# Half-masked score columns left out, with swapped token halves for the second batch entry

## The chip, the cores and the metric

The kernel runs on one core of a Trainium2 chip. A core has five engines that work side by side: TensorE (PE in the profile; matrix products, with the weight loads listed as PEld), VectorE (DVE), ScalarE (ACT), GpSimd (POOL) and SyncE (SP). TensorE writes into PSUM, of which this kernel uses eight banks of 128 x 512 float32 values; the others work on PSUM and on the on-chip SBUF. Sixteen DMA engines move data between the chip's main memory and SBUF; a load is issued by one of the engines, and in this kernel nearly all loads are issued by GpSimd[...].

The metric is device time in microseconds (us) for one launch; lower is better.

## The reference

Two layers follow each other. The first is a retention (linear attention with decay) over 4 batch entries, 8 heads, 768 tokens and 64 values per head. The second is a feed-forward block with a sigmoid gate on the 3072 token rows.

```python
# q, k, v: (4, 8, 768, 64)
gamma = 1.0 - 2.0 ** (-5.0 - np.arange(H))          # one decay per head
for t in range(S):
    state = gamma[None, :, None, None] * state + np.einsum('bhd,bhe->bhde', k[:, :, t], v[:, :, t])
    y[:, :, t] = scale * np.einsum('bhd,bhde->bhe', q[:, :, t], state)
...
x = y.transpose(0, 2, 1, 3).reshape(B * S, H * D)   # (3072, 512)
gate = 1.0 / (1.0 + np.exp(-(x @ w_gate)))          # w_gate, w_val: (512, 1536)
out = (gate * (x @ w_val)) @ w_out                  # w_out: (1536, 512)
```

The kernel doesn't step token by token. It cuts the 768 tokens into 6 chunks of 128 (C). Inside a chunk it forms the scores of each key token against each query token, multiplies them with a table that holds the decay and is zero where the key is later than the query (the causal mask), and multiplies the result with v ("intra"). What comes from earlier chunks goes through a 64 x 64 state per head ("inter").

## The kernel before

A "pair" is one chunk t of two batch entries: pair i stands for chunk i // 2 and entries 2 (i % 2) and 2 (i % 2) + 1, so there are 12 pairs. Pairs 0 and 1 have code of their own at the start; pairs 2 to 11 go through the code below. j is the entry within the pair, p one of four couples of heads, e the head within the couple. D = 64, H = 8, NP = 4, NT = 6. `half(x)` is partitions 0 to 63 or 64 to 127.

Loads, issued by GpSimd. Rows of 64 values are the unit that a load moves in these patterns. For the second entry the two heads of each couple change places, hence three loads for k and three for q.

```python
    def load_v(i):
        t, h = divmod(i, 2)
        vs[i] = ld.tile([C, 2 * H, D], BF16, tag="vs", name="vs", bufs=6)
        nc.gpsimd.dma_start(out=vs[i], in_=v[2 * h:2 * h + 2, :, t * C:(t + 1) * C, :].rearrange("b h s d -> s (b h) d"))

    def load_swapped(tiles, x, i, tag, bufs):
        t, h = divmod(i, 2)
        tiles[i] = ld.tile([C, 2 * H, D], BF16, tag=tag, name=tag, bufs=bufs)
        src = x[2 * h:2 * h + 2, :, t * C:(t + 1) * C, :].rearrange("b h s d -> b s h d")
        nc.gpsimd.dma_start(out=tiles[i][:, 0:H], in_=src[0])
        dst = tiles[i][:, H:2 * H].rearrange("s (p e) d -> s e p d", e=2)
        pairs = src[1].rearrange("s (p e) d -> s e p d", e=2)
        for e in range(2):
            nc.gpsimd.dma_start(out=dst[:, e], in_=pairs[:, 1 - e])

    def load_kq(i):
        load_swapped(kn, k, i, "kn", 6)
        load_swapped(qn, q, i, "qn", 4)
```

Tables. `maskk` is the causal mask times the decay of the key's token; `tabsk` holds the decay per key token, chunk and head.

```python
    def later_constants():
        nc.vector.tensor_scalar(tok, begin, ahead[:, 0:1], None, op0=ALU.add)
        tab_power(tok, 0, NT)
        shape = [128, NT, 2, NP]
        nc.vector.tensor_tensor(tabz, lgz.unsqueeze(1).to_broadcast(shape),
                                begin.unsqueeze(2).unsqueeze(3).to_broadcast(shape), op=ALU.mult)
# ... (later_exps: tabs and tabz go through Exp on ScalarE)
    def last_constants():
        nc.vector.tensor_scalar(causal, ahead, 0.0, None, op0=ALU.is_le)

    def later_tables():
        src = tabs[:, :, 0:NT].rearrange("s (p e) t -> s e t p", e=2)
        dst = tabsk.rearrange("s t j (p e) -> s j e t p", e=2)
        for j in range(2):
            for e in range(2):
                nc.gpsimd.tensor_copy(dst[:, j, e], src[:, e ^ j])
        for e in range(2):
            nc.gpsimd.tensor_tensor(maskk[:, e], causal.unsqueeze(1).to_broadcast([128, NP, C]),
                                    tabsk[:, 0, e, 0::2].unsqueeze(2).to_broadcast([128, NP, C]), op=ALU.mult)
```

The steps of a pair. For a product the first operand after the output is the stationary one (the weights), the second streams: its columns are what TensorE spends time on. A stationary operand of 64 partitions by 64 columns takes one quarter of the array, so four such products can run beside each other. The transposed k and q (`kqT`) come from DMA transposes (`xbar`), except for pair 2, where TensorE transposes.

```python
    def xbar(i):
        kqT[i] = at.tile([128, 2, 2, NP, C], BF16, tag="kqX", name="kqX", bufs=4)
        for which, x in enumerate((kn[i], qn[i])):
            nc.sync.dma_start_transpose(out=kqT[i][:, which].rearrange("d j p s -> d (j p) s"),
                                        in_=x.rearrange("s h d -> s (h d)"))

    def scale_k(i):
        ks[i] = ld.tile([C, 2 * H, D], BF16, tag="ks", name="ks", bufs=3)
        nc.gpsimd.tensor_tensor(ks[i], kn[i], tabsk[:, i // 2].rearrange("s j h -> s (j h)").unsqueeze(2)
                                .to_broadcast([C, 2 * H, D]), op=ALU.mult)
# ...
    def quarter_scores(i, j):

        t = kqT[i]
        sc[i, j] = (bank([128, NP, C]), bank([128, NP, C]))
        for p in range(NP):
            for g in range(2):
                for e in range(2):
                    nc.tensor.matmul(sc[i, j][e][half(g), p, :], t[half(e), 0, j, p, half(g)], t[half(e), 1, j, p, :],
                                     start=True, stop=True)

    def mask(i, j, e):
        st = stB if e else stA
        st[i, j] = at.tile([128, NP, C], BF16, tag=f"st{e}", name=f"st{e}", bufs=4)
        nc.vector.tensor_tensor(st[i, j], sc[i, j][e], maskk[:, e ^ j], op=ALU.mult)
# ...
    def intra(i, j):
        for p in range(NP):
            for e in range(2):
                st = (stA, stB)[e ^ j][i, j]
                nc.tensor.matmul(y[i, j][half(e), p, :], vs[i][:, j * H + 2 * p + e, :], st[:, p, :],
                                 start=False, stop=True, skip_group_check=True)
# ...
    def state(i):
        zz[i] = bank([128, 2, NP, D])
        for j in range(2):
            for p in range(NP):
                for e in range(2):
                    nc.tensor.matmul(zz[i][half(e), j, p, :], ks[i][:, j * H + 2 * p + e, :],
                                     vs[i][:, j * H + 2 * p + (e ^ j), :],
                                     start=(j == 0 and p == 0), stop=True, skip_group_check=True)
# ...
    def block(old, new, st=None):

        if old is not None:
            new_y(old)
            inter(old)
        for j in range(2):
            if new is not None:
                quarter_scores(new, j)
        for j in range(2):
            if old is not None:
                intra(old, j)
        if st is not None:
            state(st)
        for j in range(2):
            if old is not None:
                y_out(old, j)
        for j in range(2):
            if new is not None:
                mask(new, j, 0)
                mask(new, j, 1)
        if st is not None:
            state_sum(st)
```

Order of the program where pairs 2 to 6 come in. Every engine works through its own instructions in this order. `hold` is a one-column copy on GpSimd that keeps later loads from being issued before a pair's transposes are done. `plan` says after which group of the feed-forward products a step is put.

```python
    first_state(0)
    first_state(1)
    load_out(0)
    load_out(1)
    load_kq(2)
    load_out(2)
    load_out(3)
    load_v(2)
# ...
    def load_next(i):
        load_kq(i)
        load_v(i)

    held = const.tile([128, 1], BF16, name="held")

    def hold(i, which=1):
        nc.gpsimd.tensor_copy(held, kqT[i][:, which, 1, NP - 1, C - 1:C])

    load_next(3)
    scale_k(2)
    new_kqT(2)
    down(0, 0, 0, 6)
    transpose(2, 0)
    down(0, 1, 0, 6)
    transpose(2, 1)
    down(0, 2, 0, 6)
    for b in range(3):
        down(0, b, 6, 9)
    for j in range(2):
        quarter_scores(2, j)
        mask(2, j, 0)
        mask(2, j, 1)
    xbar(3)
    for b in range(3):
        down(0, b, 9, 12)
    scale_k(3)
    hold(3, 0)
    load_next(4)
    load_next(5)
    down(0, 3, 0, 6)
    new_y(2)
    inter(2)
    for j in range(2):
        intra(2, j)
    for j in range(2):
        y_out(2, j)
    state(2)
    state_sum(2)
    down(0, 3, 6, 12, True)
    casts(2)
# ...
    plan = {
        1: [(2, block, None, 3), (4, block, 3, None, 3), (4, xbar, 4), (4, scale_k, 4), (4, scale_k, 5), (4, hold, 4),
            (4, load_next, 6), (5, casts, 3), (7, xbar, 5), (11, block, None, 4, 4), (12, casts, 4), (12, xbar, 6), (12, scale_k, 6),
            (12, hold, 6), (12, load_next, 7), (14, block, 4, 5, 5), (16, casts, 5), (18, block, 5, 6, 6), (19, casts, 6)],
        2: [(0, xbar, 7), (0, scale_k, 7), (0, hold, 7), (0, load_next, 8), (8, block, 6, 7, 7), (10, casts, 7), (10, xbar, 8),
# ... (two blocks for each of chunks 2 to 4, with the loads of the pairs after them)
```

In the start-up, the states of pairs 0 and 1 (`first_state`) are formed by 64 products of 64 x 64 by 64 columns (line 396) and copied out of PSUM by four 128 x 256 copies (line 401). The first weight loads (line 79) bring 128 x 2 rows of 256 values each, the later ones 128 x 4.

The feed-forward products (`up` and `down`, line 411) run between these steps, and their results pass through ScalarE (sigmoid, line 437) and VectorE (gate times value, line 438).

Of the kernel before, what the change touches and what calls it, by code (L numbers as in the profile page):

```python
# [8 lines left out]
F32 = mybir.dt.float32  # L9
BF16 = mybir.dt.bfloat16  # L10
AX = mybir.ActivationFunctionType
ALU = mybir.AluOpType
# [3 lines left out]
def kernel(  # L16
# [9 lines left out]
):  # L26


    nc = tc.nc
    B, H, S, D = q.shape  # L30
    N_TOK, D_MODEL = out.shape
# [19 lines left out]

    def load_v(i):
        t, h = divmod(i, 2)
        vs[i] = ld.tile([C, 2 * H, D], BF16, tag="vs", name="vs", bufs=6)
        nc.gpsimd.dma_start(out=vs[i], in_=v[2 * h:2 * h + 2, :, t * C:(t + 1) * C, :].rearrange("b h s d -> s (b h) d"))  # L57

    def load_swapped(tiles, x, i, tag, bufs):
        t, h = divmod(i, 2)  # L60
        tiles[i] = ld.tile([C, 2 * H, D], BF16, tag=tag, name=tag, bufs=bufs)
        src = x[2 * h:2 * h + 2, :, t * C:(t + 1) * C, :].rearrange("b h s d -> b s h d")
        nc.gpsimd.dma_start(out=tiles[i][:, 0:H], in_=src[0])  # L63
        dst = tiles[i][:, H:2 * H].rearrange("s (p e) d -> s e p d", e=2)
        pairs = src[1].rearrange("s (p e) d -> s e p d", e=2)
        for e in range(2):
            nc.gpsimd.dma_start(out=dst[:, e], in_=pairs[:, 1 - e])  # L67

    def load_kq(i):
        load_swapped(kn, k, i, "kn", 6)  # L70
        load_swapped(qn, q, i, "qn", 4)

    wg = wpool.tile([128, KT, D_FF], BF16, name="wg")
    wv = wpool.tile([128, KT, D_FF], BF16, name="wv")
# [10 lines left out]
    def load_out(s):  # L85
        nc.gpsimd.dma_start(out=wo[:, s * 3:(s + 1) * 3, :],
                            in_=moe_w_out.rearrange("(n p) d -> p n d", p=128)[:, s * 3:(s + 1) * 3, :])
# [15 lines left out]
    nc.scalar.preload_act_table(AX.Exp)  # L103
    ahead = const.tile([128, C], F32, name="ahead")
    after = const.tile([128, 3, D], F32, name="after")
    tok = const.tile([128, NT], F32, name="tok")
    begin = const.tile([128, NT], F32, name="begin")
    col = const.tile([128, C], F32, name="col")
    nc.gpsimd.iota(ahead, pattern=[[-1, C]], base=0, channel_multiplier=1, allow_small_or_imprecise_dtypes=True)
# [20 lines left out]
    lgz = const.tile([128, 2, NP], F32, name="lgz")  # L130
    lsc = const.tile([128, 1], F32, name="lsc")
    ident = const.tile([128, 128], BF16, name="ident")
    causal = const.tile([128, 128], F32, name="causal")
    decay = const.tile([128, 2, 2, 2, 3 * D], F32, name="decay")
    maskk = const.tile([128, 2, NP, C], F32, name="maskk")
    tabs = const.tile([128, H, NT + 2], F32, name="tabs")
    tabsk = const.tile([128, NT, 2, H], F32, name="tabsk")
    taby = const.tile([128, NP, C], F32, name="taby")
    tabz = const.tile([128, NT, 2, NP], F32, name="tabz")
# [19 lines left out]
    def tab_power(x, lo, n):  # L159
        nc.vector.tensor_tensor(tabs_of[:, :, :, lo:lo + n], x.unsqueeze(1).unsqueeze(1).to_broadcast([128, NP, 2, n]),  # L160
                                nlg.rearrange("s e p -> s p e").unsqueeze(3).to_broadcast([128, NP, 2, n]), op=ALU.mult)
# [17 lines left out]
    nc.scalar.copy(kb[:, 4:8], kf[:, 4:8])  # L179

    def later_constants():
        nc.vector.tensor_scalar(tok, begin, ahead[:, 0:1], None, op0=ALU.add)
        tab_power(tok, 0, NT)
        shape = [128, NT, 2, NP]
        nc.vector.tensor_tensor(tabz, lgz.unsqueeze(1).to_broadcast(shape),
                                begin.unsqueeze(2).unsqueeze(3).to_broadcast(shape), op=ALU.mult)

    def later_exps():
        nc.scalar.activation(tabs, tabs, AX.Exp)
        nc.scalar.activation(tabz[:, 1:], tabz[:, 1:], AX.Exp)  # L190

    def last_constants():
        nc.vector.tensor_scalar(causal, ahead, 0.0, None, op0=ALU.is_le)

    def later_tables():
        src = tabs[:, :, 0:NT].rearrange("s (p e) t -> s e t p", e=2)
        dst = tabsk.rearrange("s t j (p e) -> s j e t p", e=2)
        for j in range(2):
            for e in range(2):
                nc.gpsimd.tensor_copy(dst[:, j, e], src[:, e ^ j])  # L200
        for e in range(2):
            nc.gpsimd.tensor_tensor(maskk[:, e], causal.unsqueeze(1).to_broadcast([128, NP, C]),
                                    tabsk[:, 0, e, 0::2].unsqueeze(2).to_broadcast([128, NP, C]), op=ALU.mult)

# [1 line left out]

    def bank(shape, dt=F32):
        return pf.tile(shape, dt, tag="ff", name="ff")  # L210

    def half(e):
        return slice(e * D, (e + 1) * D)

    def heads(t, j, p):
        return t[:, j * H + 2 * p:j * H + 2 * p + 2, :].rearrange("s h d -> s (h d)")
# [19 lines left out]
        nc.gpsimd.tensor_tensor(ks[i], kn[i], tabsk[:, i // 2].rearrange("s j h -> s (j h)").unsqueeze(2)  # L236
                                .to_broadcast([C, 2 * H, D]), op=ALU.mult)

    def scores(i, j):
        t = kqT[i]  # L240
        sc[i, j] = (bank([128, NP, C]), bank([128, NP, C]))
        for p in range(NP):
            for e in range(2):
                nc.tensor.matmul(sc[i, j][e][:, p, :], t[half(e), 0, j, p, :], t[half(e), 1, j, p, :],
                                 start=True, stop=True)

    def quarter_scores(i, j):

        t = kqT[i]
        sc[i, j] = (bank([128, NP, C]), bank([128, NP, C]))  # L250
        for p in range(NP):
            for g in range(2):
                for e in range(2):
                    nc.tensor.matmul(sc[i, j][e][half(g), p, :], t[half(e), 0, j, p, half(g)], t[half(e), 1, j, p, :],  # L254
                                     start=True, stop=True)

    def mask(i, j, e):
        st = stB if e else stA
        st[i, j] = at.tile([128, NP, C], BF16, tag=f"st{e}", name=f"st{e}", bufs=4)
        nc.vector.tensor_tensor(st[i, j], sc[i, j][e], maskk[:, e ^ j], op=ALU.mult)  # L260

    def new_y(i):
        for j in range(2):
# [46 lines left out]
    def block(old, new, st=None):  # L310

        if old is not None:
            new_y(old)
            inter(old)
        for j in range(2):
            if new is not None:
                quarter_scores(new, j)
        for j in range(2):
            if old is not None:
                intra(old, j)  # L320
# [11 lines that stand above are left out]
# [8 lines left out]
    def first_transpose(i, which, g, eng):  # L340
        tp = bank([128, 2, 2, C], BF16)
        for p in range(2):
            for r in range(2):
                for e in range(2):
                    nc.tensor.transpose(tp[half(e), p, r ^ which], (k2, q2)[which][i][:, 4 * g + 2 * p + e, r, :], ident)  # L345
        eng(kq2[i][:, which, 2 * g:2 * g + 2], tp)

    def first_scores(i, g):
        t = kq2[i]
        s = [bank([128, 2, 2, C]) for _ in range(2)]  # L350
        for p in range(2):
            for r in range(2):
                for j in range(2):
                    for e in range(2):
                        nc.tensor.matmul(s[e][half(j), p, r].rearrange("s (o p) -> s o p", o=2),  # L355
                                         t[half(e), 0, 2 * g + p, r, half(j)], t[half(e), 1, 2 * g + p, :, half(j)],
                                         start=True, stop=True)
        for e in range(2):
            st0[i, g, e] = at.tile([128, 2, 2, C], BF16, tag=f"st{e}", name=f"st{e}", bufs=4)
            d = decay[:, g, e]  # L360
            d = bass.AP(d.tensor, d.offset, [d.ap[0], d.ap[1], (D, 2), (1, C)])
            nc.vector.tensor_tensor(st0[i, g, e], s[e], d, op=ALU.mult)  # L362
# [27 lines left out]
    def first_state(i):  # L390
        zs = [bank([128, NP, D]) for _ in range(2)]
        for p in range(NP):
            for r in range(2):
                for j in range(2):
                    for e in range(2):
                        nc.tensor.matmul(zs[j][half(e ^ j), p, :], ks2[i][half(j), 2 * p + e, r, :],  # L396
                                         v2[i][half(j), 2 * p + e, r, :],
                                         start=(p == 0 and r == 0), stop=(r == 1), skip_group_check=True)
        new_za(i)
        for j in range(2):  # L400
            nc.vector.tensor_copy(za[i][:, j], zs[j])
# [102 lines left out]
    first_scores(0, 1)  # L504
    keep_on(1)
    first_transpose(1, 1, 0, dve)
    first_transpose(1, 1, 1, act)
    keep_on(1)
    first_y(0, 0)
# [22 lines left out]
    for n1 in (2, 4):  # L532
        gates = [up_part(0, wg, (n1 + i,)) for i in range(2)]
        for i in range(2):
            gate_times_val(0, (n1 + i,), 0, 512, (gates[i], up_part(0, wv, (n1 + i,))))
        if n1 == 2:
            last_constants()
            later_tables()
    first_state(0)
    first_state(1)  # L540
    load_out(0)
    load_out(1)
    load_kq(2)
    load_out(2)
    load_out(3)
    load_v(2)
    casts(0)
# [20 lines left out]
    down(0, 2, 0, 6)  # L568
    for b in range(3):
        down(0, b, 6, 9)  # L570
    for j in range(2):
        quarter_scores(2, j)
        mask(2, j, 0)
        mask(2, j, 1)
    xbar(3)
# [73 lines left out]
```

## Time and profile before

| | |
|---|---|
| time, median of 3 runs | 226.71 us (225.34 to 226.97) |
| span of the profiled execution | 223.7 us |
| granted TensorE clock | 1.00 |
| TensorE busy | 217.7 us, 97% |
| VectorE busy | 115.4 us, 52% |
| ScalarE busy | 69.3 us, 31% |
| GpSimd busy | 103.7 us, 46%, all of it before 147 us |
| score products of pairs 2 to 11 (L254) on the chain that ended last | 2.2% of the span |

The span runs from the first to the last instruction of the profile, so it is a little shorter than the measured time. In the profile, "L254" is line 254 of the kernel, and "x32" means 32 instructions. In a timeline a row gives the start, the time covered, the engine, the line, the operation with its output and inputs, the number of merged instructions, and in square brackets how long the engine had been idle and what ended that. Times of GpSimd's DMA rows are the times of issuing, not of moving the data. A group's row gives after the bar its busy time in total, the mean of one instruction in ns, and the idle time of the engine just before.

### The profile page before, as it was taken

The numbers are of one execution on the slowest core, as the hardware profiler recorded it, in microseconds if no ns is written. First come the engines' busy times: TensorE is split into PE (matmuls) and PEld (weight loads), VectorE is DVE, ScalarE is ACT, GpSimd is POOL, SyncE is SP. The second block draws the span as 40 slices with busy tenths as digits, with TensorE's granted clock in tenths as the row PEclk, the third lists the DMA queues.
The fourth block names the chain that finished last, engine by engine and source line by source line (L and its number), as shares of the span: only waits on it lengthen the run. The fifth ranks groups of instructions, "written<-read, shape, count | busy, mean of one in ns | idle before, by whom it ended". The sixth has DMA issues, their size and how long they took to land.

```text
span 223.7 us, 6625 instructions
## 1 busy us (share of the span) xinstructions
PE 217.7 (97%) x2901; PEld 129.4 (58%) x2907; DVE 115.4 (52%) x203; ACT 69.3 (31%) x116; POOL 103.7 (46%) x129
## 2 busy tenths in 40 slices
PE   7999999999999999999999999999999999999993
PEld 2565445569999656556556556555555555555553
DVE  8864653164963987936708445806335702344201
ACT  6754333243233122332222332222332322333220
POOL 8999979849965809459193190820000000000000
PEclk9999999999999999999999999999999999999999
DMA  7999999999999999969999699792600011100022
GB/s 130 176 193 197 196 187 187 156 186 176 167 135 160 115 166 148 178 63 99 119 146 149 134 86 153 51 159 77 144 0 3 0 73 71 50 1 0 3 94 97
DMA packets 99709, 25.86 MB, mean 116 GB/s; under 512 B 87648, under 2 KB 96736, under 8 KB 99680
## 3 DMA queue, kind: packets, MB, share of 16 engines
q0 software_dynamic: 75808, 13.90, 76.5%
q1 hardware_dynamic: 23200, 11.21, 25.4%
q8 instruction: 23, 0.38, 0.7%
q10 hardware_dynamic: 672, 0.33, 0.5%
q14 instruction: 6, 0.05, 0.1%
HBM read 28.31 MB, written 6.29 MB: 155 GB/s over the span
## 4 chain that ended last, share of the span: by engine, by line
PE 94%; DVE 4%; issue 0%; POOL 0%; POOLq 0%
PE ff L411 82%; PE ff L277 3%; PE ff L254 2%; PE ff L427 2%; PE ff L270 2%; DVE st L362 1%; PE ff L345 1%; PE ff L295 1%; DVE decay L151 1%; PE ff L355 1%; PE ff L225 0%; DVE kn L178 0%; PE ff L396 0%; PE ff L486 0%; DVE lgz L174 0%
## 5 line engine op out<-in xcount | busy, mean ns | idle before, releaser
L438 DVE TENSOR_TENSOR hT<-gs,ff 128x512 bf16<-128x512 f32 x72 | 48.7, 684 | 57.9 <-PE ff L411 55.6
L411 PE MATMUL ff<-xT,wv 128*64 128x512 bf16 (+2 forms) x616 | 71.9, 346 | 0.0
L411 PE MATMUL ff<-xT,wg 128*64 128x512 bf16 (+2 forms) x614 | 71.6, 346 | 0.1
L437 ACT ACTIVATE gs<-ff 128x512 f32<-128x512 f32 x72 | 42.9, 597 | 82.6 <-PE ff L411 80.9
L411 PE MATMUL ff<-wo,hT 128*64 128x512 bf16 (+3 forms) x580 | 64.6, 361 | 0.1
L411 PEld LDWEIGHTS <-wv 128*64 128x64 bf16 (+1 forms) x616 | 36.2, 109 | 24.4
L411 PEld LDWEIGHTS <-wg 128*64 128x64 bf16 (+1 forms) x616 | 35.8, 109 | 23.7
L411 PEld LDWEIGHTS <-hT 128*64 128x64 bf16 (+1 forms) x582 | 32.7, 109 | 27.1
L459 ACT COPY ob<-ff 128x512 f32<-128x512 f32 x23 | 13.5, 585 | 57.3 <-PE ff L411 57.2
L260 DVE TENSOR_TENSOR st<-ff,maskk 128x512 bf16<-128x512 f32 x40 | 24.7, 679 | 6.4 <-PE ff L254 6.4
L288 DVE TENSOR_TENSOR xT<-ff,taby 128x512 bf16<-128x512 f32 x20 | 12.9, 685 | 28.4 <-PE ff L277 28.4
L559 POOL COPY held<-kqX 128x1 bf16<-128x1 bf16 x7 | 1.3, 187 | 36.6 <-DMA kqX<-qn 33.9
L236 POOL TENSOR_TENSOR ks<-kn,tabsk 128x1024 bf16<-128x1024 bf16 x8 | 15.4, 1928 | 1.6 <-DMA kn<-in_k_dram 1.2
L67 POOL DMA_DIRECT2D qn<-in_q_dram x20 | 15.4, 794 | 0.1
L67 POOL DMA_DIRECT2D kn<-in_k_dram x20 | 15.2, 778 | 0.0
L57 POOL DMA_DIRECT2D vs<-in_v_dram x10 | 12.0, 1202 | 0.6 <-DMA wo<-in_moe_w_out_dram 0.5
L308 DVE TENSOR_TENSOR zb<-za,tabz 128x512 bf16<-128x512 f32 x10 | 11.1, 1114 | 0.2
L63 POOL DMA_DIRECT2D kn<-in_k_dram x10 | 9.2, 925 | 1.8 <-issue 1.7
L63 POOL DMA_DIRECT2D qn<-in_q_dram x10 | 9.2, 919 | 0.2 <-DMA kn<-in_k_dram 0.2
L486 PE MATMUL ff<-zero 128*128 128x512 bf16 x19 | 7.5, 534 | 1.4 <-DVE zero L141 1.2
L277 PE MATMUL ff<-st,vs 128*64 128x128 bf16 x160 | 6.4, 222 | 0.0
L79 POOL DMA_DIRECT2D wg<-in_moe_w_gate_dram x7 | 6.0, 868 | 0.0
(78 smaller groups left out, 112.5 us busy)
## 6 DMA issues: line engine op xcount, KB each, us to landing
out_dram<-ob SPq DMA_DIRECT2D x19, 256.0 KB, 2.6
vs<-in_v_dram POOLq DMA_DIRECT2D x10, 256.0 KB, 7.0
qn<-in_q_dram POOLq DMA_DIRECT2D x14, 128.0 KB, 4.9
kn<-in_k_dram POOLq DMA_DIRECT2D x12, 128.0 KB, 4.3
wo<-in_moe_w_out_dram POOLq DMA_DIRECT2D x4, 384.0 KB, 7.0
wg<-in_moe_w_gate_dram POOLq DMA_DIRECT2D x5, 256.0 KB, 6.9
wv<-in_moe_w_val_dram POOLq DMA_DIRECT2D x5, 256.0 KB, 7.5
kn<-in_k_dram POOLq DMA_DIRECT2D x20, 64.0 KB, 4.2
```

What stands on the lines that cost most here:

```text
L57: nc.gpsimd.dma_start(out=vs[i], in_=v[2 * h:2 * h + 2, :, t * C:(t + 1) * C, :].rearrange("b h s d -> s (b h) d"))
L63: nc.gpsimd.dma_start(out=tiles[i][:, 0:H], in_=src[0])
L67: nc.gpsimd.dma_start(out=dst[:, e], in_=pairs[:, 1 - e])
L236: nc.gpsimd.tensor_tensor(ks[i], kn[i], tabsk[:, i // 2].rearrange("s j h -> s (j h)").unsqueeze(2) .to_broadcast([C, 2 * H, D]), op=ALU.mult)
L260: nc.vector.tensor_tensor(st[i, j], sc[i, j][e], maskk[:, e ^ j], op=ALU.mult)
L277: nc.tensor.matmul(y[i, j][half(e), p, :], vs[i][:, j * H + 2 * p + e, :], st[:, p, :], start=False, stop=True, skip_group_check=True)
L288: nc.vector.tensor_tensor(xT[t][:, :, c:c + C], y[i, j], taby, op=ALU.mult)
L308: nc.vector.tensor_tensor(zb[i], za[i], tabz[:, i // 2 + 1].unsqueeze(3).to_broadcast([128, 2, NP, D]), op=ALU.mult)
L411: nc.tensor.matmul(o[c], w[:, c], x, **marks)
L437: nc.scalar.activation(g, ps[0], AX.Sigmoid)
L438: nc.vector.tensor_tensor(hT[t][:, n1s[0]:n1s[-1] + 1, lo:hi], g.rearrange("p (i n) -> p i n", n=n), ps[1].rearrange("p (i n) -> p i n", n ...
L459: nc.scalar.copy(ob, o)
```

## The change

Of a chunk's 128 x 128 scores per head, those with the key later than the query are zero after the mask. Split into key halves and query halves, one of the four 64 x 64 squares lies wholly behind the mask: late keys against early queries. The change doesn't compute it. For the products of late keys only the late 64 query columns are streamed.

For one entry alone this would shorten only the products of one key half, so one column half of the array would have less to do than the other. To balance the quarters, the second entry's k and v are loaded with their token halves swapped: its late keys lie in partitions 0 to 63, its early keys in 64 to 127. A sum over key tokens doesn't depend on their order, so the products with v and the state stay as they are, as long as k, v, the mask and the decay tables have the same order. q keeps its order. The two entries' score products are also interleaved.

This takes more loads (k of the second entry in four parts for two, v in three parts for one), a second mask table, a second set of decay values, and st tiles that are kept for the whole program: the square that is never written is set to zero once. The mask becomes two operations for one, on the columns 64 to 127 of all partitions, and on the columns 0 to 63 of the half with early keys.

```diff
     def load_v(i):
         t, h = divmod(i, 2)
         vs[i] = ld.tile([C, 2 * H, D], BF16, tag="vs", name="vs", bufs=6)
-        nc.gpsimd.dma_start(out=vs[i], in_=v[2 * h:2 * h + 2, :, t * C:(t + 1) * C, :].rearrange("b h s d -> s (b h) d"))
+        src = v[2 * h:2 * h + 2, :, t * C:(t + 1) * C, :].rearrange("b h s d -> b s h d")
+        nc.gpsimd.dma_start(out=vs[i][:, 0:H], in_=src[0])
+        for g in range(2):
+            nc.gpsimd.dma_start(out=vs[i][half(g), H:2 * H], in_=src[1, half(1 - g)])
# ...
         for e in range(2):
-            nc.gpsimd.dma_start(out=dst[:, e], in_=pairs[:, 1 - e])
+            for to, of in halves:
+                nc.gpsimd.dma_start(out=dst[to, e], in_=pairs[of, 1 - e])

     def load_kq(i):
-        load_swapped(kn, k, i, "kn", 6)
-        load_swapped(qn, q, i, "qn", 4)
+        load_swapped(kn, k, i, "kn", 6, ((half(0), half(1)), (half(1), half(0))))
+        load_swapped(qn, q, i, "qn", 4, ((slice(0, C), slice(0, C)),))
# ...
+    def swapped_constants():
+        for g in range(2):
+            nc.vector.tensor_scalar(tok[half(g), 1], tok[half(g), 0], float(D - 2 * g * D), None, op0=ALU.add)
+        tab_power(tok[:, 1], NT + 2, NT)
# ...
     def last_constants():
-        nc.vector.tensor_scalar(causal, ahead, 0.0, None, op0=ALU.is_le)
+        nc.vector.tensor_scalar(causal[:, 0], ahead, 0.0, None, op0=ALU.is_le)
+        for g in range(2):
+            nc.vector.tensor_scalar(causal[half(g), 1], ahead[half(g)], float(2 * g * D - D), None, op0=ALU.is_le)
# ...
+    def mask_table(j):
         for e in range(2):
-            nc.gpsimd.tensor_tensor(maskk[:, e], ...)
+            nc.gpsimd.tensor_tensor(maskk[:, j, e], ...)
+
+    sts = [[[const.tile([128, NP, C], BF16, name=f"st{r}{j}{e}") for e in range(2)] for j in range(2)] for r in range(2)]
+
+    def zero_scores():
+        for r in range(2):
+            for j in range(2):
+                for e in range(2):
+                    nc.vector.memset(sts[r][j][e][half(1 - j), :, 0:D], 0.0)
# ...
-    def quarter_scores(i, j):
+    def quarter_scores(i):
         t = kqT[i]
-        sc[i, j] = (bank([128, NP, C]), bank([128, NP, C]))
+        for j in range(2):
+            sc[i, j] = (bank([128, NP, C]), bank([128, NP, C]))
         for p in range(NP):
-            for g in range(2):
-                for e in range(2):
-                    nc.tensor.matmul(sc[i, j][e][half(g), p, :], t[half(e), 0, j, p, half(g)], t[half(e), 1, j, p, :],
-                                     start=True, stop=True)
+            for j in range(2):
+                for g in range(2):
+                    n = slice(0 if g == j else D, C)
+                    for e in range(2):
+                        nc.tensor.matmul(sc[i, j][e][half(g), p, n], t[half(e), 0, j, p, half(g)], t[half(e), 1, j, p, n],
+                                         start=True, stop=True)

     def mask(i, j, e):
-        st = stB if e else stA
-        st[i, j] = at.tile([128, NP, C], BF16, tag=f"st{e}", name=f"st{e}", bufs=4)
-        nc.vector.tensor_tensor(st[i, j], sc[i, j][e], maskk[:, e ^ j], op=ALU.mult)
+        st = (stA, stB)[e]
+        st[i, j] = sts[i % 2][j][e]
+        for rows, n in ((slice(0, C), slice(D, C)), (half(j), slice(0, D))):
+            nc.vector.tensor_tensor(st[i, j][rows, :, n], sc[i, j][e][rows, :, n], maskk[rows, j, e, :, n], op=ALU.mult)
# ... in the order of the program:
     first_transpose(1, 1, 0, dve)
+    swapped_constants()
     first_transpose(1, 1, 1, act)
# ...
             last_constants()
+            zero_scores()
             later_tables()
+            mask_table(0)
# ...
     load_kq(2)
     load_out(2)
+    mask_table(1)
     load_out(3)
     load_v(2)
```

## The prediction

> **What bounds the kernel now.** I read the page's first two parts, then the waits, then TensorE's and GpSimd's timelines against each other.
>
> ```profile
> PE 217.7 (97%) x2901; PEld 129.4 (58%) x2907; DVE 115.4 (52%) x203; ACT 69.3 (31%) x116; POOL 103.7 (46%) x129
> ...
> PE   7999999999999999999999999999999999999993
> ...
> POOL 8999979849965809459193190820000000000000
> ...
> DMA  7999999999999999969999699792600011100022
> ```
>
> TensorE is full from the second slice (5.6 us each) to the last, so a column that it doesn't stream is time gained, and any wait put before it is time lost. GpSimd and the DMA engines are also nearly full, but only in the first half: there the loads are issued. In the list of waits TensorE's matmuls wait 1.2 us for one memset at the start and under 1 us for all else together. So nothing holds TensorE up today, and what matters is how near each supplier comes to being late. These two lists, GpSimd's timeline and then TensorE's, show the near places:
>
> ```profile
> 27.64 1.52 POOL L67 DMA_DIRECT2D kn<-in_k_dram  x2
> ...
> 31.95 0.75 POOL L86 DMA_DIRECT2D wo<-in_moe_w_out_dram  x1 [0.40 <-DMA wo<-in_moe_w_out_dram]
> 33.88 0.76 POOL L86 DMA_DIRECT2D wo<-in_moe_w_out_dram  x1 [1.19 <-DMA wo<-in_moe_w_out_dram]
> 34.73 1.18 POOL L57 DMA_DIRECT2D vs<-in_v_dram  x1
> ...
> 42.31 1.92 POOL L236 TENSOR_TENSOR ks<-kn,tabsk 128x1024 bf16<-128x1024 bf16 x1
> ...
> 49.09 0.19 POOL L559 COPY held<-kqX 128x1 bf16<-128x1 bf16 x1 [2.77 <-DMA kqX<-kn]
> ...
> 69.07 0.19 POOL L559 COPY held<-kqX 128x1 bf16<-128x1 bf16 x1 [3.31 <-DMA kqX<-qn]
> ...
> 83.79 0.19 POOL L559 COPY held<-kqX 128x1 bf16<-128x1 bf16 x1 [6.08 <-DMA kqX<-qn]
> ```
>
> ```profile
> 47.94 0.42 PE L295 MATMUL ff<-vs,ks 128*64 128x64 bf16 x16
> ...
> 54.82 0.64 PE L254 MATMUL ff<-kqX 64*64 64x128 bf16 x32
> ...
> 72.40 0.64 PE L254 MATMUL ff<-kqX 64*64 64x128 bf16 x32
> ...
> 84.28 0.66 PE L254 MATMUL ff<-kqX 64*64 64x128 bf16 x32
> ```
>
> The scaled keys of pair 2 (L236) are done at 44.2 and used by its state product (L295) at 47.94: slack 3.7 us. The tiny copies "held" mark when a pair's transposed keys and queries are there. Pair 4: 69.07 against its scores at 72.40, slack 3.3. Pair 6: 83.79 against 84.28, slack 0.5. Later pairs: 97.5 against 103, 110.8 against 117.5, slack 5 and more.
>
> The costs come from the table of groups (busy total, mean ns):
>
> ```profile
> L260 DVE TENSOR_TENSOR st<-ff,maskk 128x512 bf16<-128x512 f32 x40 | 24.7, 679 | 6.4 <-PE ff L254 6.4
> L67 POOL DMA_DIRECT2D kn<-in_k_dram x20 | 15.2, 778 | 0.0
> L57 POOL DMA_DIRECT2D vs<-in_v_dram x10 | 12.0, 1202 | 0.6 <-DMA wo<-in_moe_w_out_dram 0.5
> L63 POOL DMA_DIRECT2D kn<-in_k_dram x10 | 9.2, 925 | 1.8 <-issue 1.7
> ```
>
> **What the Trainium skill says.** "TensorEngine Tiling (Array Packing)", Instruction Overhead, says that below about 60 columns a matmul gets no shorter. The change stops at 64, and the trace has 64x64 products of 64 columns: 64 of L396 take 0.67 us on the chain, 10.5 ns each. "DMA: Bandwidth & Descriptors", Rules for kernel authors, advises against two transfers to disjoint partition halves, as both use the same 16 engines; the change does just that. This trace has no split pair of that kind, but it shows that an issue is paid mostly by the piece (below). "VectorE: DVE Perf Modes", the section on the TRN2 errata, says that small operations pay a fixed latency each. The trace agrees: 128x256 copies out of PSUM (L401) average 0.414 us, 128x512 products 0.679.
>
> **Part 1: TensorE's columns.** A pair's scores are 32 products on four 64x64 quarters of the array, so 8 x 128 = 1024 columns per quarter. L411 streams 24 x 512 columns in 5.18 us at 78.9, that is 0.42 ns a column: 1024 cost 0.43 us, and the chain shows 0.45. With half of the products at 64 columns, and both entries interleaved with opposite halves short, each quarter streams 4 x (128 + 64) = 768, so 0.32 us. By issue, 32 x 10.5 ns = 0.34, so the floor hardly bites. Saved: 0.10 us x 10 pairs = **1.0 us**, all of it on the path.
>
> **Part 2: VectorE.** A pair's mask becomes 8 operations of 256 columns for 4 of 512. Back to back, the 512 ones start every 0.60 us (4 in 2.48), the 256 ones of L401 every 0.33 (4 in 1.41): 2.7 for 2.5 us, +0.2 per pair, off the path, since VectorE is half idle. Eight memsets and two extra comparisons at 23 us: some 0.15 to 0.25 us each (estimate from the 128x256 memset at 272 ns), 1.5 to 2.5 us in a gap of 2.09 us, which PSUM's spare banks cover. The three small operations at 11.4 us: about 0.4 us in a gap of 0.51. I charge 0 to 0.2 us.
>
> **Part 3: GpSimd.** Issuing costs 1.18, 0.90 and 0.735 us from start to start at 2048, 1024 and 512 rows (v; half of a pair; one parity of L67). The slope, 0.28 per 1024 rows, gives 0.68 at 256 rows; the first two weight loads, with 256 rows, start every 0.70. So k changes from 0.90 + 2 x 0.735 to 0.90 + 4 x 0.70: **+1.33**. v from 1.18 to 0.90 + 2 x 0.735: **+1.19**. Per pair 2.5 us, over ten pairs 25 us more issue. The second mask table adds two multiplications, **+2.15** as for the first, ahead of pair 2's v.
>
> **Part 4: a limit on loads in flight.** Each of the four DMA waits of GpSimd between 31 and 58 us (the two of wo, v of pair 3, q of pair 5) ends at the landing of the issue exactly eight places back. With k cut finer, the two last pieces of pair 2's q fall eight after the first two wo loads. They'd issue at 31.95 and 33.88, where wo waits now.
>
> **Adding up at the first place.** After that q at 34.6: wo 0.8, mask table 2.15, wo 0.8, v of pair 2 2.4, pair 3's k 3.7, q 2.4, v 2.4 give 49.2; the scaling of pair 2 ends at 51.1. TensorE is there at 47.9: it **stalls 3.2 us** (1.5 with no waits for landings, 4 with one more).
>
> **At the second place.** Scaling pair 3 ends at 53.1; pair 3's k, issued by 44.5 for 38.25 now, lands transposed near 54 for 49.1. TensorE wants it at 54.8 + 3.2, so no stall. Two loads of 6.1 + 2.5 take 17 us: 71.2. Two scalings: 75.2. The hold of pair 4 finds its data ready, so pair 6's load starts near 76, for 69.5 now: 6.5 later. Its k costs 1.33 more, and 0.5 slack comes off: pair 6's scores start **7.3 us** after today's time. That includes the 3.2, since these are times by GpSimd's clock, not stalls to be added. Pair 5 in between comes near 79, wanted at 80.7. Later pairs: a load gains 1.3 before its transposes, slack is 5 to 7 and the holds wait 5 to 8, so no further loss.
>
> Sum: +7.3 at pair 6, which the six shorter score blocks up to there do not reduce, as the wait absorbs them; -0.5 for the five after it. That is +6.8; some latency should shrink, as the DMA engines are less crowded when issue is slower (landing took 7 to 9 us between 46 and 70 us, 4 after). I take off 0.8: 226.7 + 6.0 = **232.7 us**.
>
> **Rivals.** (a) Loads are bound by the DMA engines, not by issue: they show 9 tenths there, and q and v of pairs 4 and 5 take 7 to 9 us to land. Bytes and row sizes are unchanged, so later issue would only shorten the backlog. Then only part of the delay reaches pair 6: +1 to +3, 228 to 230. Against it: the scaling of pair 2 waits for GpSimd's own turn, not for data. (b) Everything stays hidden, and the columns gained show: 225.7. For it, 33.9 us of hold waits on GpSimd, 3 to 8 each. Against it, the first slack is 3.7 us and at least 5 are added before it. (c) The finer loads meet the eight-places limit often and pair 7 or 8 stalls too: 236 to 240. Against it, the holds there are long.
>
> **Range and chances.** Between (a) and the low end of (c): 228.5 to 237. The 2% mark is 231.2; my sum with 1.5 us less still passes it. Slower by over 2%: 0.68; within 2%: 0.29; faster by over 2%: 0.03, as the whole column saving is 0.5%.
>
> **What would show it.** Right: score blocks of 32 at 0.32 to 0.36 us on the chain; k's issues of 0.70 each; TensorE waiting for POOL at the first L295-type block near 48 to 51 us; pair 6's scores near 91 us, behind a DMA wait; none later. Wrong: no wait of TensorE on POOL or kqX, or issues of 256 rows that cost 0.4 us, or score blocks that stay at 0.45 because short products don't pack.

## The result and the profile after

The changed kernel takes 232.24 us (median of 4 runs, 231.74 to 233.34), against 226.58 for the kernel before beside it: a ratio of 1.027, 95% interval 1.0223 to 1.0317. It is 5.7 us slower. The span of the profiled execution grew from 223.7 to 230.0 us.

The page of the changed kernel, the same lines as before and the granted TensorE clock:

```profile
PE 219.8 (96%) x2907; PEld 129.7 (56%) x2907; DVE 121.0 (53%) x256; ACT 69.4 (30%) x116; POOL 127.0 (55%) x171
...
PE   7999999948999999999999999999999999999993
...
POOL 8999969799996992963949658192000000000000
PEclk9999999997999999999999999999999999999999
DMA  8999999999999999998999979999500012100022
```

TensorE's row has a hole in the ninth and tenth of the 40 slices (46 to 57.5 us), and in the tenth the clock row falls to 7. GpSimd (POOL) is busy for 127.0 us instead of 103.7. The waits of TensorE's matmuls (us in total, times, longest):

```profile
PE ff L315 <- POOL ks L260: 3.9, 1, 3.9
...
PE ff L430 <- DMA wo<-in_moe_w_out_dram: 0.3, 1, 0.3
PE ff L273 <- DMA kqX<-qn: 0.3, 1, 0.3
```

L315 is the state product, L260 the scaling of the keys, L273 the scores, L430 the feed-forward products. One wait stands out. TensorE's timeline places it and shows what follows:

```profile
52.68 0.44 PE L315 MATMUL ff<-vs,ks 128*64 128x64 bf16 x16 [3.90 <-POOL ks L260]
52.96 1.80 PE L430 MATMUL ff<-wo,hT 128*64 128x512 bf16 x12
54.54 1.92 PE L430 MATMUL ff<-xT,wg 128*64 128x256 bf16 x16
56.25 1.59 PE L430 MATMUL ff<-xT,wv 128*64 128x256 bf16 x16
57.67 1.04 PE L430 MATMUL ff<-xT,wg 128*64 128x256 bf16 x16
...
61.26 0.54 PE L273 MATMUL ff<-kqX 64*64 64x128 bf16 x32
...
90.89 0.74 PE L273 MATMUL ff<-kqX 64*64 64x128 bf16 x32 [0.30 <-DMA kqX<-qn]
```

The same stretch in the kernel before, right after its state product:

```profile
48.19 1.47 PE L411 MATMUL ff<-wo,hT 128*64 128x512 bf16 x12
49.49 1.04 PE L411 MATMUL ff<-xT,wg 128*64 128x256 bf16 x16
50.36 1.04 PE L411 MATMUL ff<-xT,wv 128*64 128x256 bf16 x16
51.23 1.04 PE L411 MATMUL ff<-xT,wg 128*64 128x256 bf16 x16
```

After the pause a group of 16 products takes 1.92 and 1.59 us, and only from 57.67 on its usual 1.04. From 52.96 to 57.67 TensorE does in 4.71 us what took 3.04 before (48.19 to 51.23). The table by stretches says why; the third number from the end is the granted clock:

```profile
52.00:54.00 2.00, 1.32 (x26) 0.85 (x28) 0.80 (x2) 0.00 (x0) 2.00 (x2) 0.99 2.14 159
54.00:56.00 2.00, 2.00 (x18) 1.43 (x16) 1.05 (x1) 0.59 (x1) 2.00 (x4) 0.50 0.99 263
56.00:58.00 2.00, 2.00 (x28) 1.76 (x25) 0.05 (x1) 0.60 (x1) 2.00 (x4) 0.66 0.90 142
```

The clock was 0.50 and 0.66, which made TensorE 1.7 us later still. GpSimd's timeline shows what led to the pause:

```profile
28.43 2.48 POOL L75 DMA_DIRECT2D kn<-in_k_dram  x4
...
32.01 0.76 POOL L75 DMA_DIRECT2D qn<-in_q_dram  x1 [0.21 <-issue]
34.63 0.75 POOL L75 DMA_DIRECT2D qn<-in_q_dram  x1 [1.86 <-DMA wo<-in_moe_w_out_dram]
...
36.13 2.05 POOL L219 TENSOR_TENSOR maskk<-causal,tabsk 128x512 f32<-128x512 f32 x2
...
44.71 0.61 POOL L75 DMA_DIRECT2D kn<-in_k_dram  x1 [0.76 <-DMA wo<-in_moe_w_out_dram]
46.05 0.89 POOL L70 DMA_DIRECT2D qn<-in_q_dram  x1 [0.73 <-DMA vs<-in_v_dram]
...
50.66 3.83 POOL L260 TENSOR_TENSOR ks<-kn,tabsk 128x1024 bf16<-128x1024 bf16 x2
...
76.78 0.22 POOL L582 COPY held<-kqX 128x1 bf16<-128x1 bf16 x1
...
90.88 0.18 POOL L582 COPY held<-kqX 128x1 bf16<-128x1 bf16 x1 [4.00 <-DMA kqX<-qn]
```

The scaling of pair 2 starts at 50.66 (42.31 before), after the finer loads, the second mask table and the waits for landings. The copy at 76.78 no longer waits at all: before, it stood at 69.07 after a wait of 3.31. Pair 6's data is there at 90.88 (83.79 before), and TensorE, which comes only 0.3 us earlier, starts pair 6's scores at 90.89 (84.28 before). That start sets the time: from it to the last piece of the chain it is 135.0 to 135.7 us in the profiles of the kernel before, of the changed kernel (three) and of the kernels below with a filled wait (three). The costs, mean of one in ns:

```profile
L280 DVE TENSOR_TENSOR st<-ff,maskk 128x256 bf16<-128x256 f32 x80 | 30.1, 415 | 7.0 <-PE ff L273 6.5
...
L75 POOL DMA_DIRECT2D kn<-in_k_dram x40 | 25.0, 660 | 0.8 <-DMA wo<-in_moe_w_out_dram 0.8
...
L64 POOL DMA_DIRECT2D vs<-in_v_dram x20 | 14.4, 762 | 0.0
```

And the gain, on the chain that ended last: pair 7's score block before and after.

```profile
102.94 0.45 PE ff L254 x32
...
109.64 0.35 PE ff L273 x17
```

### The profile page after: what moved, and what is told of

The parts are those of the page before. It is cut to its first block, busy times and chain, and to the rows that moved or that the text cites. A ratio compares the mean times of both kernels' runs of the same rounds, so it can differ in the third digit from the quotient of the medians.

```text
span 230.0 us, 6738 instructions
## 1 busy us (share of the span) xinstructions
PE 219.8 (96%) x2907; PEld 129.7 (56%) x2907; DVE 121.0 (53%) x256; ACT 69.4 (30%) x116; POOL 127.0 (55%) x171
## 4 chain that ended last, share of the span: by engine, by line
PE 64%; DMA 15%; POOL 15%; issue 2%; DVE 2%; POOLq 0%; SPq 0%; DVEq 0%
PE ff L430 56%; DMA qn<-in_q_dram 4%; DMA kn<-in_k_dram 3%; DMA wo<-in_moe_w_out_dram 3%; DMA vs<-in_v_dram 3%; POOL ks L260 3%; POOL kn L75 2%; DMA kqX<-qn 2%; POOL maskk L219 2%; PE ff L297 2%; POOL qn L75 2%; POOL vs L64 2%; PE ff L446 2%; DVE sf L381 1%; POOL vs L62 1%
## 5 line engine op out<-in xcount | busy, mean ns | idle before, releaser
L457 DVE TENSOR_TENSOR hT<-gs,ff 128x512 bf16<-128x512 f32 x72 | 48.8, 686 | 57.5 <-PE ff L430 54.9
L430 PE MATMUL ff<-xT,wg 128*64 128x512 bf16 (+2 forms) x616 | 72.8, 350 | 0.0
L430 PE MATMUL ff<-xT,wv 128*64 128x512 bf16 (+2 forms) x616 | 72.4, 348 | 0.0
L430 PE MATMUL ff<-wo,hT 128*64 128x512 bf16 (+3 forms) x582 | 65.2, 363 | 0.3 <-DMA wo<-in_moe_w_out_dram 0.3
L430 PEld LDWEIGHTS <-wv 128*64 128x64 bf16 (+1 forms) x616 | 36.7, 111 | 24.6
L430 PEld LDWEIGHTS <-wg 128*64 128x64 bf16 (+1 forms) x616 | 36.3, 111 | 24.1 <-issue 0.4
L430 PEld LDWEIGHTS <-hT 128*64 128x64 bf16 (+1 forms) x582 | 32.7, 109 | 27.6 <-DVE hT L457 0.4
L280 DVE TENSOR_TENSOR st<-ff,maskk 128x256 bf16<-128x256 f32 x80 | 30.1, 415 | 7.0 <-PE ff L273 6.5
L308 DVE TENSOR_TENSOR xT<-ff,taby 128x512 bf16<-128x512 f32 x20 | 12.9, 686 | 25.3 <-PE ff L297 25.3
L75 POOL DMA_DIRECT2D kn<-in_k_dram x40 | 25.0, 660 | 0.8 <-DMA wo<-in_moe_w_out_dram 0.8
L75 POOL DMA_DIRECT2D qn<-in_q_dram x20 | 15.7, 820 | 2.1 <-DMA wo<-in_moe_w_out_dram 1.9
L260 POOL TENSOR_TENSOR ks<-kn,tabsk 128x1024 bf16<-128x1024 bf16 x8 | 15.7, 1986 | 0.0
L64 POOL DMA_DIRECT2D vs<-in_v_dram x20 | 14.4, 762 | 0.0
L62 POOL DMA_DIRECT2D vs<-in_v_dram x10 | 9.5, 953 | 2.0 <-DMA kn<-in_k_dram 2.0
L70 POOL DMA_DIRECT2D kn<-in_k_dram x10 | 9.4, 943 | 1.4 <-issue 1.4
L70 POOL DMA_DIRECT2D qn<-in_q_dram x10 | 9.6, 957 | 0.7 <-DMA vs<-in_v_dram 0.7
L505 PE MATMUL ff<-zero 128*128 128x512 bf16 x21 | 8.2, 522 | 1.2 <-DVE zero L149 1.2
L328 DVE TENSOR_TENSOR zb<-za,tabz 128x512 bf16<-128x512 f32 x10 | 8.4, 852 | 0.2
L324 DVE TENSOR_TENSOR za<-za,ff 128x512 f32<-128x512 f32 x8 | 5.5, 686 | 3.5 <-PE ff L315 3.3
```

The lines of the kernel that those rows point to most:

```text
L62: nc.gpsimd.dma_start(out=vs[i][:, 0:H], in_=src[0])
L64: nc.gpsimd.dma_start(out=vs[i][half(g), H:2 * H], in_=src[1, half(1 - g)])
L75: nc.gpsimd.dma_start(out=dst[to, e], in_=pairs[of, 1 - e])
L280: nc.vector.tensor_tensor(st[i, j][rows, :, n], sc[i, j][e][rows, :, n], maskk[rows, j, e, :, n], op=ALU.mult)
L308: nc.vector.tensor_tensor(xT[t][:, :, c:c + C], y[i, j], taby, op=ALU.mult)
L328: nc.vector.tensor_tensor(zb[i], za[i], tabz[:, i // 2 + 1].unsqueeze(3).to_broadcast([128, 2, NP, D]), op=ALU.mult)
```

## The experiments

Each was run beside the kernel before on one chip. Ratios are to that kernel, with the 95% interval.

**Whole loads in the changed kernel.** What the changed kernel would be if its finer loads cost nothing; it leaves out the swap of the halves in the data, so the second entries' output isn't the reference's.

```diff
-    load_swapped(kn, k, i, "kn", 6, ((half(0), half(1)), (half(1), half(0))))
+    load_swapped(kn, k, i, "kn", 6, ((slice(0, C), slice(0, C)),))
     # and v in one load, as before
```

> The changed kernel with the loads of k and v as they were before (the token halves are not swapped in the data; everything else of the change stays, so the second entries' result is left out as a result). Issue theory (the finer loads make GpSimd late): GpSimd is about 2.5 us per pair shorter, no wait of TensorE on the scaled keys or on transposed keys, 226.6 - 1.0 for the columns + 0.4 at the start = 226.0, 225.3 to 226.8. Rival (VectorE's doubled mask operations or the short products cost the time): 230 or more, nearly as the changed kernel.

Measured: 225.66 us, 0.9982 (0.9957 to 1.0007). TensorE's waits for scaled and transposed keys are gone, with the second mask table and all of VectorE's and TensorE's changes still in. On the chain the score blocks take 0.35 or 0.47 us, where they took 0.45 or 0.57 before:

```profile
103.05 0.35 PE ff L270 x17
```

So the loads cause the loss, and neither the doubled mask operations nor the short products do. It also shows the ceiling: 0.1 us a pair, 1 us for ten pairs, of which about 0.5 is lost at the start, where TensorE is that much later in this profile than in the one of before. A gain over the kernel before is not shown, as the interval reaches 1.

**Finer loads alone.** The kernel before with k in five loads and v in three, each part to its own place.

```diff
-            nc.gpsimd.dma_start(out=dst[:, e], in_=pairs[:, 1 - e])
+            for part in parts:
+                nc.gpsimd.dma_start(out=dst[part, e], in_=pairs[part, 1 - e])
# ...
-        load_swapped(kn, k, i, "kn", 6)
+        load_swapped(kn, k, i, "kn", 6, (slice(0, D), slice(D, C)))
# ... (q with one part, and v in three loads)
```

> The kernel before with nothing changed but the loads, cut as finely as in the change (each part to its own place, so nothing is swapped and the result is the reference's). Issue theory: the second mask table is missing (2.1 us less on GpSimd), so the scaled keys of pair 2 come near 50 us, TensorE waits some 2 us there, pair 6's scores start near 89 us: 229.5 to 231.5. Rival (mask operations or short products): 226.6, as before.

Measured: 229.92 us, 1.0155 (1.0099 to 1.021). TensorE waits in both foreseen places:

```profile
PE ff L299 <- POOL ks L240: 2.7, 1, 2.7
...
PE ff L258 <- DMA kqX<-qn: 1.0, 1, 1.0
```

Pair 6's scores start at 88.53. So the finer loads alone cost 3.7 us, without the gain of the change and without its second mask table. The clock stays at 1.00 after the 2.7 us pause, which ends at 50.99:

```profile
52.00:54.00 2.00, 2.00 (x36) 1.69 (x34) 1.31 (x2) 0.94 (x2) 1.00 (x3) 1.00 1.54 233
```

**Pair 2's scaling moved to VectorE.**

```diff
-    scale_k(2)
+    scale_k(2, nc.vector)
```

> The changed kernel with the scaling of pair 2's keys done by VectorE, which is idle there, in place of GpSimd. GpSimd is 1.9 us shorter before pair 6's load, and the 3.9 us wait of the state product goes. Gate theory (pair 6's transposed keys and queries are late by GpSimd's own clock, whatever TensorE does before): the wait comes back at pair 6, 4 us or so, and the time falls by only 1.9: 230.3, 229.5 to 231. Stall theory (the wait at pair 2 and the lower TensorE clock after it are the loss): it falls by 3.9 to 5.6, to 226.6 to 228.3.

Measured: 1.014 (1.0052 to 1.0228), some 229.4 us, at the edge of the gate theory's range and with an interval that reaches into both; two of its four runs, the profiled one among them, were disturbed and are not in that ratio, so the profile is read for the waits alone:

```profile
54.97 0.18 POOL L582 COPY held<-kqX 128x1 bf16<-128x1 bf16 x1 [1.92 <-DMA kqX<-kn]
...
57.40 0.54 PE L273 MATMUL ff<-kqX 64*64 64x128 bf16 x32 [1.75 <-DMA kqX<-qn]
...
91.09 0.54 PE L273 MATMUL ff<-kqX 64*64 64x128 bf16 x32 [4.36 <-DMA kqX<-qn]
```

The wait at pair 2 is gone and comes back at pairs 3 and 6, as the gate theory has it. But pair 6's data (91.09, for 90.88 in the changed kernel) didn't get earlier by GpSimd's saved 1.9 us: GpSimd then waited 1.92 us at pair 3's hold. That hold needs both the end of the scalings, which it followed without a wait in the changed kernel (54.38), and the transposed keys of pair 3, whose loads are issued before the scalings. Both come at almost the same time there, so taking one away gains nothing.

**The wait filled.** 17 products on zeros in front of pair 2's state product.

```diff
+    keep_on(17)
     state(2)
```

> The changed kernel with 17 products on zeros (3.6 us) put where TensorE waits for pair 2's scaled keys; nothing else changes. Clock theory (the clock of 0.68 after the wait is part of the loss): the clock stays at 1.0, TensorE reaches pair 6 1.6 us sooner and the whole time falls by that, to 230.6. Gate theory: the clock stays at 1.0, but TensorE then waits some 1.7 us longer at pair 6, and the time stays at 231.8 to 232.6.

Measured: 229.91 us, 1.015 (1.0105 to 1.0195). That is 2.3 us under the change's 232.24, but the two didn't run side by side, so they do in the next pair.

> The changed kernel once more, so that the filled wait stands beside it on one chip: 231 to 232.5.

> The 17 products on zeros in the wait for pair 2's scaled keys, now beside the changed kernel on one chip. Clock theory: 1.3 to 2 us faster than the changed kernel, 229.5 to 230.5. Gate theory (pair 6 takes all of it back): within 0.4 us of the changed kernel.

Measured on one chip: the changed kernel 231.65 us, 1.0213 (1.0171 to 1.0255); with the wait filled 229.59, 1.0135 (1.0099 to 1.0171). That is 2.1 us less by the medians, 1.8 by the ratios. The same stretches as above, with the wait filled:

```profile
52.00:54.00 2.00, 2.00 (x36) 1.19 (x36) 1.28 (x2) 0.02 (x1) 1.63 (x1) 1.00 1.78 164
54.00:56.00 2.00, 2.00 (x42) 2.00 (x38) 0.40 (x2) 1.16 (x2) 1.77 (x4) 1.00 1.09 357
56.00:58.00 2.00, 2.00 (x42) 2.00 (x38) 0.94 (x2) 0.60 (x1) 2.00 (x4) 1.00 1.03 128
```

TensorE does more work and ends sooner, with the clock at 1.00. So it was the idle time that brought the clock down, and the time fell as the clock theory says. The way to it is another, though. In both profiles TensorE still pauses before pair 6's scores, 0.59 us with the wait filled and 0.64 in the changed kernel beside it. The profile names a VectorE operation that ended 0.1 us earlier, but the scores start as the hold shows the data landed:

```profile
89.02 0.18 POOL L582 COPY held<-kqX 128x1 bf16<-128x1 bf16 x1 [3.99 <-DMA kqX<-qn]
```

In the changed kernel that was at 90.54, so the difference is in the landing of pair 6's data. It came at 88.53 and 89.02 in the two profiles with the wait filled, and at 90.88, 89.29 and 90.54 in the three of the changed kernel. Why a fuller TensorE should bring it forward isn't settled. The gain from filling is shown; that it is the clock's is not.

**Half of the wait filled**, with the changed kernel beside it.

> The changed kernel itself, beside the runs below on one chip. As on record: 231.7 to 233.3; a wait of TensorE of about 4 us for pair 2's scaled keys, then some 4 us at a clock of 0.5 to 0.7.

```diff
+    keep_on(8)
     state(2)
```

> The changed kernel with 8 products on zeros (1.7 us) put into the 4 us wait for pair 2's scaled keys, so that TensorE idles for about 2.2 us there. If the clock falls only after a long pause (the kernel with finer loads alone paused 2.7 us and kept 1.0): the clock stays at 1.0 and the time is that of the filled wait, 2 us under the changed kernel, 229.5 to 230.5. If any pause of that place costs clock: 231.5 or more, as the change.

Measured: the changed kernel 231.2 us, 1.0203 (1.0133 to 1.0273); half filled 230.46, 1.0181 (1.0119 to 1.0243). The times overlap, so the expected gain of time isn't shown. The clock's part is. After the 1.7 us of pause that were left, the clock is at 1.00:

```profile
52.00:54.00 2.00, 1.68 (x30) 1.06 (x32) 1.16 (x2) 0.00 (x0) 2.00 (x2) 1.00 1.56 178
```

In the changed kernel beside it, it is at 0.94, 0.50 and 0.76 around and after a pause of 3.65 us:

```profile
48.00:52.00 4.00, 0.65 (x24) 0.48 (x16) 1.29 (x2) 0.00 (x0) 4.00 (x5) 0.94 1.58 132
52.00:54.00 2.00, 1.71 (x22) 0.98 (x24) 0.99 (x2) 0.00 (x0) 2.00 (x2) 0.50 3.27 134
54.00:56.00 2.00, 2.00 (x26) 1.41 (x23) 0.66 (x1) 0.58 (x1) 1.52 (x4) 0.76 1.23 301
```

What the clock gave was taken back: TensorE waited 0.54 us for pair 5's data and 1.31 for pair 6's, which landed at 90.61 in this profile.

**Columns left out without a swap.** Late keys of both entries in the same partitions, loads as before.

```diff
-                    n = slice(0 if g == j else D, C)
+                    n = slice(0 if g == 0 else D, C)
```

> The columns behind the mask left out without the swap: both entries' late keys lie in the same partitions, loads and mask table as before, mask in two operations, the result is the reference's. If quarters have to balance: the quarters with the early keys still stream 1024 columns a pair, the score blocks stay at 0.45 us, and the time stays at 226.2, 225.5 to 226.8. If only the sum of columns counts: blocks of 0.35 us and 225.2.

Measured: 226.67 us, 1.0014 (0.9991 to 1.0037). The blocks last as long as before (0.63, where the change has 0.54; both with the last product's tail):

```profile
55.51 0.63 PE L268 MATMUL ff<-kqX 64*64 64x128 bf16 x32
```

So the balance is needed: a quarter of the columns fewer, but not in the fullest quarters, is worth nothing.

**The swap without finer loads of k.** The transposed keys have their tokens along the free dimension, so the swap of k is only an index (`half(g ^ j)` for the stationary operand). v is swapped by two copies within SBUF, issued by SyncE, and VectorE makes the second mask table in its gap.

```diff
-                        nc.tensor.matmul(sc[i, j][e][half(g), p, n], t[half(e), 0, j, p, half(g)], t[half(e), 1, j, p, n],
+                        nc.tensor.matmul(sc[i, j][e][half(g), p, n], t[half(e), 0, j, p, half(g ^ j)], t[half(e), 1, j, p, n],
# ... (k and v loaded whole; in the new swap_v, called after the transposes of a pair)
+        for g in range(2):
+            nc.sync.dma_start(out=vx[i][half(g)], in_=vs[i][half(1 - g), H:2 * H])
```

> The change without its finer loads: k is loaded whole and the token halves are swapped by taking the other half of the transposed keys as stationary operand; v is loaded whole, and SyncE copies the second entry's halves crosswise within SBUF for the product with the scores; the second mask table and the zeros are made by VectorE in its 6 us gap at 38 to 44 us; no constants at the start. Issue theory: no wait of TensorE at pair 2, the score blocks at 0.35 us, 225.5, 224.8 to 226.0: up to 1 us under the kernel before, less what pair 6's transposed keys (0.5 us early today) give back. Rival (the swap costs whatever does it, for instance by the added copies on crowded DMA engines): over 227.

Measured: 229.18 us, 1.0143 (1.0076 to 1.0211). It falls to the rival. Pair 2's copied v is late:

```profile
49.84 0.41 PE L308 MATMUL ff<-st,vx 128*64 128x128 bf16 x8 [1.42 <-DMA vx<-vs]
```

The mask table's two multiplications on VectorE took 0.68 and 3.30 us; the second, from 42.2 to 45.5, ran in the time in which GpSimd scaled the keys of pairs 2 and 3 (42.4 to 44.4, and from 45.0). And TensorE shows a pause of 1.21 us before 75.6 that the profile puts down to no supplier.

**v loaded twice.** k as in the last; the swapped v comes by two more loads, issued where GpSimd waits anyway; the mask table in VectorE's gaps at 31 to 37 us, away from GpSimd's multiplications.

```diff
# ... in swap_v, issued by GpSimd and no longer by SyncE:
+        for g in range(2):
+            lo = i // 2 * C + (1 - g) * D
+            nc.gpsimd.dma_start(out=vx[i][half(g)], in_=v[2 * (i % 2) + 1, :, lo:lo + D, :].rearrange("h s d -> s h d"))
```

> The change with k loaded whole (halves swapped by index of the transposed keys), v loaded whole for the state and the second entry's v a second time with swapped halves, in two loads that are issued where GpSimd would wait anyway or after the loads that pairs 3 and 6 need; the second mask table by VectorE in the gaps of its 28 to 37 us. Issue theory: pair 2's scaled keys come near 46 us, no wait there; pair 6 as before or some tenths late: 225.8, 225.0 to 226.8, level with the kernel before or 0.5 us under it. If the added 0.26 MB a pair crowd the DMA engines so that a transpose comes late: 227 to 229.

Measured: 229.25 us, 1.0152 (1.01 to 1.0204). Pair 2 waits for nothing and the mask table costs 0.68 us an operation, but pair 6 is late again:

```profile
87.03 0.76 PE L287 MATMUL ff<-kqX 64*64 64x128 bf16 x32 [1.46 <-DMA kqX<-qn]
```

Pair 4's hold moved from 69.07 to 70.92 and still waits for a landing, 1.44 us. That the added bytes, on DMA engines that are at 9 tenths there, delay the landings fits this, but no run shows it alone. No version that gives the reference's result beat the kernel before.

## Why the prediction was right

The time, 232.24 for 232.7, and the main steps are right: the loads' issue makes GpSimd late, and TensorE pays at pair 2 and at pair 6. The changed kernel's later measurements, 231.2 (1.0203) and 231.65 (1.0213), lie up to 1 us lower, so the loss is 2.0 to 2.7%. By its own steps:

- **Columns**: foreseen 0.32 us a block by columns and 0.34 by issue, measured 0.35 for 0.45; 0.10 us a pair. Without the balance, nothing.
- **VectorE**: the eight mask operations take 3.06 us, foreseen 2.7, and stay off the path. At the start TensorE was 0.4 us late, where 0 to 0.2 was charged. The kernels without the new constants at the start are 0.6 late there (v copied, v loaded twice) or 0.1 (finer loads alone), with waits for the first k in all three and for q in two of them; so I don't put it down to the constants.
- **GpSimd's issue**: mis-sized. 256 rows start every 0.62 us (4 in 2.48), foreseen 0.70, and a pair costs some 2.0 us more for 2.5. In return the waits eight places back grew: 1.86 at pair 2's q, as foreseen, and 0.76, 0.73 and 1.97 more. In the kernel with finer loads alone the waits for landings took back part of what the missing mask table saved: pair 3's hold came only 0.6 us earlier (53.79 for 54.38) for 2.05 us of work taken out.
- **First place**: the stall was foreseen as 3.2 and measured as 3.9, 3.65 and 3.78 in three profiles. The scaled keys came 1.5 us later than reckoned, by the 0.76 and 0.73, and TensorE 0.8 us later.
- **Second place**: right in its path, as pair 6's data sets the time. It was foreseen 7.3 us later, or 6.5 with the 0.8 taken off for shorter landings; measured 6.6 (90.89 for 84.28). Within that, two errors cancel: pair 6's load began 0.9 us later than reckoned (76.90 for 76), and from there the data took 14.0 us, less than the 14.3 of before although k's issue alone takes 1 us longer.
- **What I had wrong there** is TensorE's wait: some 4 us by my sum, and in fact 0.3, since TensorE itself came late. It was 0.8 us late before the first place, paused 3.9, and lost 1.7 to its clock, a term that is missing from my sum. The Trainium skill has it, in "TensorE: Matmul & The Clock Gate", section "What's actually happening": after an idle window of about 3.4 us the clock is halved. These runs agree in the main: pauses of 1.7 and 2.7 us keep 1.00, 3.65 to 3.9 give 0.50, each time for 3.4 us (2 + 1.36 + 0.04 us by the first table, and likewise by the one beside the half fill). But the latter's 0.94 puts the fall at 51.5, when TensorE had been idle for only 2.9 us. I read the size of the stall and didn't ask what a stall of that size does.
- **Rivals**: (a) asked for +1 to +3 us and is refuted as a whole, though landings stand close behind GpSimd's own work, as the moved scaling shows; (b) is refuted by the finer loads alone; (c) did not happen: later pairs show no wait, and the delay shrinks by 0.1 us with each score block after pair 7.

So the close agreement is partly luck: cheaper issue, more waits for landings and shorter landings happen to balance. The lost clock cost the whole kernel little in these profiles. Pair 6's scores start at 90.89, 89.62 and 90.55 in the three of the changed kernel, and the data landed at 90.88, 89.29 and 90.54: an earlier TensorE would have waited for it. With the wait filled the loss is 3.5 us (229.59 for 226.06) and the data lands at 88.5 to 89.0; what brings it there is the open end of this case.

## What to carry to other kernels

Before cutting a load finer, count issues and not only bytes: at 0.6 to 0.7 us for even a 32 KB piece, two more pieces of k and two of v cost GpSimd twenty times the 0.1 us that they brought TensorE per pair. A swap can also be had from an operand that is addressed freely (here the transposed keys), but expect little where the DMA engines are full: both versions that did so were still 1.4 and 1.5% slower than the kernel before. Find the wait that ends last before mending an earlier one: here the start of pair 6 set the time, and a filled or removed wait at pair 2 showed only as far as it moved that. When a full TensorE has to stall, look at its clock afterwards: 2.7 us kept it here, 3.65 us halved it, and 17 products on zeros in the gap kept it and made the kernel some 2 us faster.

## What the hardware showed unexpectedly

TensorE's clock fell to 0.50 for 3.4 us with a single pause of 3.65 to 3.9 us, and cost TensorE up to 1.7 us of work. A float32 multiplication of 128 x 512 on VectorE took 3.30 us while GpSimd multiplied, and 0.68 when GpSimd only issued loads. The kernel before has it too: its product of the state with the decay table (L308, 128 x 512 from SBUF) takes 3.08 us at 89.63 and 1.97 at 76.30, where GpSimd scales keys, and 0.69 at 82.79, where it doesn't; the masks, which read PSUM, start every 0.60 us at 43.74 beside the same scalings. Which rule is behind this was not tested. In three kernels TensorE paused once for 1.2, 1.5 and 0.65 us in the midst of feed-forward products with no supplier named (v copied within SBUF, the columns without a swap, v loaded twice); what it waited for stays open.
